# Attention and FFN on one core: the values product in parts between the two heads' transposes, scores of both heads first

## The chip, the core and the metric

One core of a Trainium2 chip runs the whole program. The time is device microseconds from launch to end; the median of three runs is compared. The span in a profile is the time between the first and the last instruction of one profiled execution.

## What is computed

Multi-head attention (batch 4, 8 heads, 576 positions, head width 64) with a position bias from a small network, then per batch a feed-forward layer with a convolution over three positions and a gate:

```python
scores = scale * q @ k.T + bias[h, i, j]        # bias = relu(x[i,j] * w1 + b1) @ w2
attn   = softmax(scores)                        # over j
x      = attn @ v                               # heads side by side: 4 x 576 x 512
h      = relu(x @ w_in)                         # 512 -> 1024
out    = (h * sigmoid(conv3(h))) @ w_out        # 1024 -> 512
```

All is float32 in and out.

## The kernel before

There are three stages: the bias table is computed and written to DRAM (to about 65 us in the profile), the attention runs (to about 328 us), then the feed-forward layer.

**Sequences and units.** The attention works on 16 sequences n, one for each pair of heads p and batch b. A sequence has five units, named by their row tile t, in the order t = 1, 2, 3, 4, 0 (`units`); below they are unit 0 to unit 4 by their place ui in that order. Units 0 to 3 hold 128 query rows for each of two heads h; unit 4 (t = 0) holds the remaining 64 rows of both heads in one tile. The loop `for u, (n, t) in enumerate(flat)` near the end of the printed code is software-pipelined over units: in pass u it issues

- `scores` of unit u+2 for head h: on TensorE (L341) into a PSUM tile `s` (pool psS, two tiles), then on VectorE (L348) the bias sum and the row minimum in one instruction, into `sp` and `nm`;
- `expo` of unit u+1 for head h: ScalarE's exponential (L362);
- `transposes` of unit u for head h: TensorE (L397) turns the 128 x 576 block into two PSUM tiles `tp` (pool psT, three tiles), one of which ScalarE copies to `pt` and the other VectorE (L88 and L91). ScalarE writes two columns of `sr` (L323) ahead of the first head's transposes.

**The values product.** When a group of row tiles is complete, `pv_parts` puts five parts on the list `fill`; a part is one block of 128 keys, both heads, and is two matmuls (L441) that accumulate in PSUM, 256 columns wide for a group of two tiles and 64 for unit 4's group. After the last part ScalarE copies the sum to `x` (L88). How many parts a pass takes off the list, at its end, is the table `pv_share`.

**Normalising.** `invert(n-1)` gives the reciprocals of the row sums on VectorE; two more transposes (L404) in unit 2 turn them, VectorE copies them to `rt`, and `normalise` sends them over the SyncE queue (SP) to DRAM (`r_d`, L472 to L474) and back, spread over partitions (`rb`, L477). At the end of unit 4 GpSimd (POOL) multiplies `x` by `rb` (L483).

**Weights beside it.** Each weight piece of the feed-forward layer is a job of `job_steps`, whose steps are called after each head's transposes over two units: L96 on ScalarE and L97 on VectorE, L99, L103, then GpSimd splits the piece (L130, L131). L97 of a job writes a buffer that GpSimd's L131 of the job before has to have read. A job's L97 falls into every second unit: for even n into unit 1 of the next sequence after GpSimd's L483, for odd n into unit 2.

**Loads.** All go over SP, in the order of the code: `load(n+2)` (queries and keys, four DMAs of 928 KB in all, L149 and L150) in unit 2, after the last scores of sequence n; `load_v` (values, four DMAs of 448 KB, L164 to L167) into one of two fixed tiles; the weight pieces (L118); and in every fourth sequence the five bias tiles of the next pair of heads (L175, L177). The DMAs take eight completion semaphores in turn, so one waits for the eighth before it to land.

Of the kernel before, what the change touches and what calls it, by code (L numbers as in the profile page):

```python
# [19 lines left out]
def attention_ffn_kernel(  # L20
# [63 lines left out]
    NSEQ = len(seq)  # L84
# [5 lines left out]
    def dve(o, i):  # L90
        nc.vector.tensor_copy(o, i)  # L91
# [25 lines left out]
    def load_w(raw, src):  # L117
        nc.sync.dma_start(raw.rearrange("p n t -> p (n t)"), src.bitcast(I32))  # L118
# [14 lines left out]
    with tc.manual_schedule():  # L133
# [27 lines left out]
        def load_v(n):  # L161
            p, b = seq[n]
            vts[n] = vt = v_t[n % 2]
            nc.sync.dma_start(vt[0:TL, 1:], v[b, p, 0:TL])  # L164
            nc.sync.dma_start(vt[TL:P, 6:], v[b, p, TL:P, 5:])
            nc.sync.dma_start(vt[TL:P, 1:5], v[b, p, TL:P, 0:4])
            nc.sync.dma_start(vt[TL:P, 0], v[b, p, TL:P, 4])  # L167
# [153 lines left out]
        def turned_sp(n, t):  # L321
            tile = sp_p.tile([P, 2 * S + 2], F32R, name="sr", tag=spt[n, t][1])
            nc.scalar.activation(tile[:, 2 * S:], pars[:, 0:2], AF.Copy)  # L323
            spt[n, t] = (tile, None)
# [34 lines left out]
        def expo(n, t, h):  # L359
            sp, nm = spt[n, t][0], nms[n, t]  # L360
            col = 4 * h + t - 1 if t else 8
            exps[n, t, h] = nc.scalar.activation(  # L362
                sp[:, h], sp[:, h], AF.Exp, bias=nm[:, h:h + 1], scale=-1.0,
                accum_out=sms[n][:, col:col + 1],
            )
# [3 lines left out]
        def group(n, t):  # L369
            return t if n == 0 and t > 2 else (t + 1) // 2  # L370

        def ends_group(n, t):
            return t in (0, 2, 4) or n == 0 and t == 3

        def transposes(n, t, h, sums=None):
            g = group(n, t)
            if (n, g) not in ptt:
                ptt[n, g] = pt_p.tile([P, 9, 2 * P], F32, name="pt") if g else pt0s[n % 2]
            pt = ptt[n, g]
            c0 = P if t == 2 or t == 4 and n else 0  # L380
            if h == 0:
                turned_sp(n, t)
            spf = spt[n, t][0]


            last = h or not t
            rows = P if t else TL
            blocks = [(4 * h + c, (5 * h + c) * P, P) for c in range(4)]
            if last:
                blocks.insert(4 - 4 * h, (8 if t else 4, NM, P if n or t else TL))  # L390


            ps = [psT.tile([P, 512], F32, name="tp").rearrange("p (c x) -> p c x", x=TL) for _ in range(2)]
            halves_ = [slice(TL * a, TL * a + TL) for a in range(2)]
            for k, (bk, j, cols) in enumerate(blocks):
                for a, ra in enumerate(halves_):
                    tr = nc.tensor.transpose(  # L397
                        ps[a][0:cols, bk - 4 * h].bitcast(F32R), spf[ra, j:j + cols], identr[ra, ra]
                    )
                    if k == 0 and a == 0:  # L400
                        tc.add_manual_dep(tr.ins, exps.pop((n, t, h)).ins.name, DATA)
            if sums is not None:
                for a, ra in enumerate(halves_):
                    nc.tensor.transpose(ps[a][:, 5], rr_t[sums % 2][ra], ident[ra, ra])  # L404
            for a, copy in ((0, act), (1, dve)):
                cs = slice(c0 + TL * a, c0 + TL * a + TL)
                if rows == P:
                    copy(pt[:, 4 * h:4 * h + len(blocks), cs], ps[a][:, 0:len(blocks)])
                else:
                    copy(pt[:, 0:4, cs], ps[a][:, 0:4])  # L410
                    copy(pt[0:rows, 4, cs], ps[a][0:rows, 4])
            if sums is not None:
                rts[sums] = r_p.tile([9, P], F32, name="rt")
                for a, ra in enumerate(halves_):
                    dve(rts[sums][:, ra], ps[a][0:9, 5])
# [81 lines left out]
        def ffn_in(b, f):  # L497
            ps = psS.tile([P, 2, 512], F32, name="s")
            cs = slice(f * P, f * P + P)
            i = 0  # L500
            for c in range(KC):
                for pw, px in ((0, 0), (0, 1), (1, 0)):
                    for a in range(2):
                        nc.tensor.matmul(  # L504
                            ps[:, a, 0:HS],
                            wi[c][:, pw, cs],
                            xss[b, c][:, px, a * HS:(a + 1) * HS],
                            start=(i == 0),
                            stop=(i == 3 * KC - 1),
                        )  # L510
                    i += 1
            if (b, f) in ((0, 0), (0, 1)):
                h = e_p.tile([P, S], F32, name="h")
            else:
                h = g_p[0].tile([P, S], F32, name="h", tag="g")
            nc.scalar.activation(halves(h), ps[:, :, 0:HS], AF.Relu)  # L516
            return h
# [35 lines left out]
        def heads(t):  # L553
            return (0, 1) if t else (0,)

        fill = deque()
# [42 lines left out]
        for u in range(2):  # L599
            for h in heads(flat[u][1]):  # L600
                scores(*flat[u], h)
            if u == 0:
                for h in heads(flat[0][1]):
                    expo(*flat[0], h)
        pv_share = (5, 0, 5, 0, 5)
        rb = None
        hs_ff = {}
        raw_w = {}
        job_steps = iter(())
# [3 lines left out]
        for u, (n, t) in enumerate(flat):  # L613
            p, b = seq[n]
            ui = units.index(t)
            for h in range(2):
                if u + 2 < NU:
                    if h in heads(flat[u + 2][1]):
                        scores(*flat[u + 2], h)
                if u + 1 < NU and h in heads(flat[u + 1][1]):  # L620
                    expo(*flat[u + 1], h)
                if h in heads(t):
                    transposes(n, t, h, n - 1 if h and ui == 2 and n else None)
                next(job_steps, None)
            del spt[n, t]
            if u + 2 >= NU:
                f = u + 2 - NU
                hs_ff[0, f] = ffn_in(0, f)
            if u == 1 or n and ui == 2 and n + 2 < NSEQ:
                load(2 if u == 1 else n + 2)  # L630
            if ui == (1 if n > 1 else 3) and 1 <= n and n + 1 < NSEQ:
                load_v(n + 1)
            if u in conv_weights:
                conv_weights[u]()

            for at, do in ((u - 8, "load"), (u - 11, "split")):
                job = at // 2
                if at % 2 == 0 or not 0 <= job < 4 * KC + 2 * FE:
                    continue
                if job < 4 * KC:  # L640
                    src, dst = w_in[job // 4 * P:job // 4 * P + P], wi[job // 4]
                else:
                    src, dst = w_out[(job - 4 * KC) // 2 * P:(job - 4 * KC) // 2 * P + P], wo[(job - 4 * KC) // 2]
                cs = slice(job % 4 * 256, job % 4 * 256 + 256) if job < 4 * KC else slice(job % 2 * 256, job % 2 * 256 + 256)
                if do == "load":
                    raw_w[job] = e_p.tile([P, 256, 2], I32, name="raw_w", tag="h")
                    load_w(raw_w[job], src[:, cs])
                else:
                    job_steps = split_w_steps(e_p, dst[:, :, cs], raw_w.pop(job), ("cv", "cv"))
            if u + 2 < NU:  # L650
                n2, t2 = flat[u + 2]
                p2, b2 = seq[n2]
                if b2 == B - 1 and p2 + 1 < NP:
                    load_bias(p2 + 1, t2)
            if ui == (0 if n > 1 else 1) and n > 0:
                invert(n - 1)

            parts = len(fill) if u < 4 else pv_share[ui]
            while fill and parts > 0:
                fill.popleft()()  # L660
                parts -= 1
            if ui == 2 and n > 0:
                rb = normalise(n - 1)
            if ends_group(n, t):
                fill.extend(pv_parts(n, group(n, t)))
            if ui == 4 and n > 0:
                apply_norm(n - 1, rb)
            if n == NSEQ - 2 and ui > 1:
                x_parts(0, ui - 2)
            if n == NSEQ - 1 and ui == 0:  # L670
                x_parts(0, 3)
            if n == NSEQ - 1 and ui in (1, 2):
                load_wo(FE - 1 + ui)
# [84 lines left out]
        for i, (b, f) in enumerate(steps):  # L758
# [12 lines left out]
            for c in range(KC):  # L771
# [5 lines left out]
                lambda f, gi, t=t: gs[b, f][:, gi, t * P:(t + 1) * P] for t in range(NT)  # L777
# [98 lines left out]
```

## Time and profile before

| | |
|---|---|
| runs (three) | 537.38 us median, 532.86 to 539.75 |
| profiled execution | 535.1 us, its span 533.3 us |
| mean granted TensorE clock | 0.991 |
| attention's full stretch on TensorE, 80 to 320 us | 225.59 us of 240 busy |
| ScalarE, VectorE, GpSimd over the span | 58%, 72%, 19% busy |

A row of the timeline reads: start, duration, engine, line, operation, output<-inputs, partitions x elements, count of records merged, and in brackets the engine's idle time just before with what ended it. A float32 matmul stands as two records. A matmul's end is modelled and overlaps the next one's start, so the cost of a step on TensorE is taken from start to start.

### The profile page before, as it was taken

What the parts mean: (1) busy time and instruction counts of PE and PEld (TensorE: products, weight loads), DVE (VectorE), ACT (ScalarE), POOL (GpSimd) and SP (SyncE); (2) the same over time, 40 slices, a digit from 0 to 9 for tenths busy, and PEclk for the clock granted to TensorE, in tenths of its full rate; (3) what the DMA queues carried; (4) which work ended last, traced back from release to release, by engine and by line L of the source; (5) the groups of instructions that cost most, each with busy time, mean ns of one, the idle gap of its engine ahead of it and who ended that gap; (6) DMA issues with size and microseconds to landing.
All of it is one profiled execution on the core that took longest, in us unless ns stands there. A gap on an engine that the chain in (4) does not pass through costs nothing.

```text
span 533.3 us, 11854 instructions
## 1 busy us (share of the span) xinstructions
PE 498.9 (94%) x4542; PEld 382.3 (72%) x4542; DVE 386.1 (72%) x919; ACT 311.6 (58%) x813; POOL 103.3 (19%) x123
## 2 busy tenths in 40 slices
PE   5989999999899999999889999899999999999995
PEld 2333466776667766677666678888998899899984
DVE  6999685677768777878678853995699169928910
ACT  6888785687757777677676654562362035215510
POOL 1000000012221222212222521562016001500000
PEclk9999999999989999999999999989999999999999
DMA  6689644597656976569754121000200200020011
GB/s 168 248 244 352 233 118 125 144 279 188 159 135 148 293 178 164 144 162 296 177 140 116 58 76 42 8 1 3 77 2 0 80 22 0 1 81 0 1 39 61
DMA packets 32707, 63.50 MB, mean 119 GB/s; under 512 B 5490, under 2 KB 11146, under 8 KB 32650
## 3 DMA queue, kind: packets, MB, share of 16 engines
q1 hardware_dynamic: 32506, 62.66, 41.1%
q8 instruction: 36, 0.59, 0.5%
q14 instruction: 21, 0.17, 0.1%
q10 hardware_dynamic: 144, 0.08, 0.1%
HBM read 46.74 MB, written 15.98 MB: 118 GB/s over the span
## 4 chain that ended last, share of the span: by engine, by line
PE 57%; DMA 11%; ACT 7%; DVE 6%; POOL 2%; issue 2%; SPq 1%; POOLq 0%; DVEq 0%; ACTq 0%
PE s L504 17%; PE tp L727 14%; PE o L441 10%; PE s L341 7%; PE tp L397 5%; PE o L727 4%; ACT sp L362 3%; DMA qk<-in_qk_dram 3%; DMA r_d<-rt 3%; DMA rb<-r_d 3%; DMA bt<-bias_d 2%; ACT pt L88 2%; POOL x L483 1%; DVE cv L702 1%; DVE sp L348 1%
## 5 line engine op out<-in xcount | busy, mean ns | idle before, releaser
L348 DVE CUSTOM_DVE_ANT_0 sp<-s,bt 128x576 f32<-128x576 f32 x144 | 107.8, 750 | 50.6 <-PE s L341 41.2
L397 PE MATMUL tp<-identr,sr 64*128 64x64 f32 x1312 | 110.7, 265 | 14.0 <-ACT pt L88 7.6
L341 PE MATMUL s<-qk 64*128 64x288 f32 x640 | 119.3, 449 | 1.2 <-DVE nm L348 1.1
L362 ACT ACTIVATE sp<-sp,nm 128x576 f32<-128x576 f32 x144 | 110.9, 770 | 3.5 <-DVE nm L348 3.4
L397 PEld LDWEIGHTS tp<-identr,sr 64*128 64x128 f32 x1312 | 78.3, 136 | 42.3 <-ACT pt L88 20.4
L504 PE MATMUL s<-xs,wi 128*128 128x288 f32 x768 | 105.2, 299 | 2.7 <-ACT h L516 2.7
L504 PEld LDWEIGHTS s<-xs,wi 128*128 128x128 f32 x768 | 104.1, 191 | 3.4 <-ACT h L516 2.9
L441 PE MATMUL o<-pt,vt 128*64 128x256 f32 (+2 forms) x940 | 88.6, 336 | 0.7 <-ACT x L88 0.7
L88 ACT ACTIVATE pt<-tp 128x256 f32<-128x256 f32 (+2 forms) x160 | 59.3, 381 | 39.0 <-PE tp L397 38.0
L441 PEld LDWEIGHTS o<-pt,vt 128*64 128x64 f32 x940 | 53.4, 138 | 26.9 <-issue 6.5
L91 DVE COPY pt<-tp 128x256 f32<-128x256 f32 (+2 forms) x160 | 66.5, 424 | 7.3 <-PE tp L397 6.8
L727 PE MATMUL tp<-wo,g 128*128 128x512 f32 x288 | 70.1, 389 | 0.0
L341 PEld LDWEIGHTS s<-qk 64*128 64x128 f32 x640 | 54.1, 185 | 19.6 <-issue 6.1
L702 DVE SCALAR_TENSOR_TENSOR cv<-h,cw,cv 128x575 f32<-128x575 f32 x64 | 60.8, 950 | 2.4 <-ACT cv L697 0.4
L727 PEld LDWEIGHTS tp<-wo,g 128*128 128x128 f32 x288 | 53.8, 188 | 11.0
L483 POOL TENSOR_TENSOR x<-x,rb 128x576 f32<-128x576 f32 x16 | 22.8, 1423 | 184.7 <-DMA rb<-r_d 169.3
L260 PE MATMUL s<-y,pars 128*32 128x512 f32 (+8 forms) x352 | 46.0, 494 | 4.6 <-ACT st L286 2.0
L243 DVE TENSOR_SCALAR y<-tl,inv,nb 128x512 f32<-128x512 f32 (+8 forms) x116 | 49.9, 502 | 0.0
L516 ACT ACTIVATE h<-s 128x576 f32<-128x576 f32 x32 | 20.8, 650 | 47.2 <-PE s L504 47.1
L708 ACT ACTIVATE cv<-cv 128x576 f32<-128x576 f32 x32 | 21.8, 682 | 29.5 <-DVE cv L702 29.5
L260 PEld LDWEIGHTS s<-y,pars 128*32 128x32 f32 x352 | 15.2, 111 | 28.9 <-DVE y L243 13.6
L130 POOL TENSOR_SCALAR xs<-x 128x576 fp32r<-128x576 f32 x16 | 15.3, 954 | 82.0 <-PE s L504 82.0
(66 smaller groups left out, 456.5 us busy)
## 6 DMA issues: line engine op xcount, KB each, us to landing
qk<-in_qk_dram SPq DMA_DIRECT2D x32, 320.0 KB
bt<-bias_d SPq DMA_DIRECT2D x32, 288.0 KB
bias_d<-st SPq DMA_DIRECT2D x14, 607.0 KB
qk<-in_qk_dram SPq DMA_DIRECT2D x32, 144.0 KB
rb<-r_d SPq DMA_DIRECT2D x32, 144.0 KB
out_dram<-o SPq DMA_DIRECT2D x17, 256.0 KB
raw_w<-in_moe_w_in_dram SPq DMA_DIRECT2D x16, 256.0 KB
vt<-in_v_dram SPq DMA_DIRECT2D x16, 224.0 KB
```

What stands on the lines that cost most here:

```text
L88: nc.scalar.activation(o, i, AF.Copy)
L91: nc.vector.tensor_copy(o, i)
L243: nc.vector.tensor_scalar(y, dist[:, 0:n], inv[:, ig:ig + 1], nb1, op0=ALU.mult, op1=ALU.max)
L260: nc.tensor.matmul(ps[32 * j:32 * j + 32, a // 512 if n > 512 else blk % 2, 0:min(n - a, 512)], w2b, ys[j][:, a:min(n, a + 512)], start=Tr ...
L341: nc.tensor.matmul(ps[:, a, 0:HS], qt[rows, qo:qo + P], qt[rows, KO + hh * HS:KO + hh * HS + HS], start=(i == 0), stop=(i == len(ops) - 1),)
L348: nc.vector.tensor_tensor_reduce(out=halves(spt[n, t][0][:, h]), in0=ps[:, :, 0:HS], in1=halves(bt[:, h]), op0=ALU.add, op1=ALU.min, scale ...
L362: exps[n, t, h] = nc.scalar.activation(sp[:, h], sp[:, h], AF.Exp, bias=nm[:, h:h + 1], scale=-1.0, accum_out=sms[n][:, col:col + 1],)
L397: tr = nc.tensor.transpose(ps[a][0:cols, bk - 4 * h].bitcast(F32R), spf[ra, j:j + cols], identr[ra, ra])
L441: nc.tensor.matmul(po[hs, oc], vt[:, slot, :], rhs, start=(c == 0), stop=(c == 4))
L504: nc.tensor.matmul(ps[:, a, 0:HS], wi[c][:, pw, cs], xss[b, c][:, px, a * HS:(a + 1) * HS], start=(i == 0), stop=(i == 3 * KC - 1),)
L702: nc.vector.scalar_tensor_tensor(out=cv[:, o:o + S - 1], in0=h[:, i:i + S - 1], scalar=cw[:, f, kk:kk + 1], in1=cv[:, o:o + S - 1], op0=AL ...
L727: nc.tensor.matmul(ps, lhs(f, gi), wo[f][:, wj, cs], start=(f == 0 and i == 0), stop=(f == FC - 1 and i == 2),)
```

## The change

For each pass the scores of both heads of unit u+2, and the exponentials of both heads of unit u+1, are issued first. Then come the first head's transposes, then the pass's parts of the values product, then the second head's transposes. The product's parts go 2, 5, 3, 2, 3 to units 0 to 4 instead of 5, 0, 5, 0, 5. For n > 1 the values are loaded in unit 2 instead of unit 1, behind `load(n+2)` and the bias, ahead of `normalise`. Nothing is computed differently.

```diff
-        pv_share = (5, 0, 5, 0, 5)
+        pv_share = (2, 5, 3, 2, 3)
...
             for h in range(2):
                 if u + 2 < NU:
                     if h in heads(flat[u + 2][1]):
                         scores(*flat[u + 2], h)
                 if u + 1 < NU and h in heads(flat[u + 1][1]):
                     expo(*flat[u + 1], h)
-                if h in heads(t):
-                    transposes(n, t, h, n - 1 if h and ui == 2 and n else None)
-                next(job_steps, None)
+            transposes(n, t, 0)
+            next(job_steps, None)
+
+            parts = len(fill) if u < 5 else pv_share[ui]
+            while fill and parts > 0:
+                fill.popleft()()
+                parts -= 1
+            if t:
+                transposes(n, t, 1, n - 1 if ui == 2 and n else None)
+            next(job_steps, None)
...
-            if ui == (1 if n > 1 else 3) and 1 <= n and n + 1 < NSEQ:
-                load_v(n + 1)
...
             if ui == (0 if n > 1 else 1) and n > 0:
                 invert(n - 1)
-
-            parts = len(fill) if u < 4 else pv_share[ui]
-            while fill and parts > 0:
-                fill.popleft()()
-                parts -= 1
+            if ui == (2 if n > 1 else 3) and 1 <= n and n + 1 < NSEQ:
+                load_v(n + 1)
             if ui == 2 and n > 0:
                 rb = normalise(n - 1)
```

TensorE, units 0 and 1 of one sequence, before (`s` scores, `tp` transposes, `o` the values product; x2 is one head's scores, x10 five parts):

```order
L341 MATMUL s<-qk 128x288 x2
L397 MATMUL tp<-identr,sr 128x64 x8
L341 MATMUL s<-qk 128x288 x2
L397 MATMUL tp<-identr,sr 128x64 x10
L441 MATMUL o<-pt_161,vt_107 64x64 x10
L341 MATMUL s<-qk 128x288 x2
L397 MATMUL tp<-identr,sr 128x64 x8
L341 MATMUL s<-qk 128x288 x2
L397 MATMUL tp<-identr,sr 128x64 x10
```

The same two units on TensorE now:

```order
L341 MATMUL s<-qk 128x288 x4
L397 MATMUL tp<-identr,sr 128x64 x8
L441 MATMUL o<-pt,vt_107 64x256 x4
L397 MATMUL tp<-identr,sr 128x64 x10
L341 MATMUL s<-qk 128x288 x4
L397 MATMUL tp<-identr,sr 128x64 x8
L441 MATMUL o<-pt_161,vt_107 64x64 x10
L397 MATMUL tp<-identr,sr 128x64 x10
```

Both units now have a piece of the product between their two sets of transposes, where before only the scores of the second head stood.

ScalarE in unit 1, before (`sp` exponentials, `pt` copies of the transposes, `u` a step of a weight job):

```order
L362 ACTIVATE sp,sm<-sp,nm 128x576
L323 ACTIVATE sr<-pars 128x2
L88 ACTIVATE pt<-tp 128x4x64
L96 ACTIVATE u<-raw_w 128x256
L362 ACTIVATE sp,sm<-sp,nm 128x576
L88 ACTIVATE pt<-tp 128x5x64
```

The same unit on ScalarE now (`x` is the copy of the short product, which stood at the end of unit 0):

```order
L362 ACTIVATE sp,sm<-sp,nm 128x576 x2
L323 ACTIVATE sr<-pars 128x2
L88 ACTIVATE pt<-tp 128x4x64
L88 ACTIVATE x_1585<-o 128x64
L88 ACTIVATE pt<-tp 128x5x64
```

The copy of the first head's transposes stands behind two exponentials instead of one, and no exponential is left between the two copies.

SP from unit 1 to unit 2 of a sequence, before (`vt` values, `qk` queries and keys, `r_d` the reciprocals on their way to DRAM):

```order
L164 DMA vt_107<-in_v_dram 64x896
L165 DMA vt_107<-in_v_dram 64x576
L166 DMA vt_107<-in_v_dram 64x256
L167 DMA vt_107<-in_v_dram 64x64
L149 DMA qk<-in_qk_dram 64x1280
L150 DMA qk<-in_qk_dram 64x2x288
L149 DMA qk<-in_qk_dram 64x1280
L150 DMA qk<-in_qk_dram 64x2x288
L118 DMA raw_w<-in_moe_w_in_dram 128x512
L472 DMA r_d<-rt 4x128
L473 DMA r_d<-rt 4x128
L474 DMA r_d<-rt 2x1x64
```

The same twelve on SP now:

```order
L149 DMA qk<-in_qk_dram 64x1280
L150 DMA qk<-in_qk_dram 64x2x288
L149 DMA qk<-in_qk_dram 64x1280
L150 DMA qk<-in_qk_dram 64x2x288
L118 DMA raw_w<-in_moe_w_in_dram 128x512
L164 DMA vt_107<-in_v_dram 64x896
L165 DMA vt_107<-in_v_dram 64x576
L166 DMA vt_107<-in_v_dram 64x256
L167 DMA vt_107<-in_v_dram 64x64
L472 DMA r_d<-rt 4x128
L473 DMA r_d<-rt 4x128
L474 DMA r_d<-rt 2x1x64
```

The four loads of the values have moved from ahead of the queries and keys to just ahead of the reciprocals.

## Rows read from the trace of the kernel before

**Rows 1.** The page's first part: each engine's busy time, share of the span and number of instructions.

```profile
PE 498.9 (94%) x4542; PEld 382.3 (72%) x4542; DVE 386.1 (72%) x919; ACT 311.6 (58%) x813; POOL 103.3 (19%) x123
```

**Rows 2.** Timeline of TensorE: the values product in unit 2, of sequence 2 and of sequence 15 (the first and the last of 14).

```profile
98.14 2.38 PE L441 MATMUL o<-pt,vt 128*64 128x256 f32 x20
...
313.18 2.38 PE L441 MATMUL o<-pt,vt 128*64 128x256 f32 x20
```

**Rows 3.** Timeline of TensorE in one sequence, from the product in unit 2 of sequence 9 to the same place of sequence 10.

```profile
214.56 2.38 PE L441 MATMUL o<-pt,vt 128*64 128x256 f32 x20
216.86 0.76 PE L341 MATMUL s<-qk 64*128 64x288 f32 x4
217.24 0.64 PE L397 MATMUL tp<-identr,sr 64*128 64x64 f32 x8
217.72 0.75 PE L341 MATMUL s<-qk 64*128 64x288 f32 x4
218.09 0.84 PE L397 MATMUL tp<-identr,sr 64*128 64x64 f32 x10
218.69 0.75 PE L341 MATMUL s<-qk 64*128 64x288 f32 x3
...
219.73 0.82 PE L341 MATMUL s<-qk 64*128 64x288 f32 x4
220.48 2.38 PE L441 MATMUL o<-pt,vt 128*64 128x256 f32 x20
...
224.67 0.58 PE L397 MATMUL tp<-identr,sr 64*128 64x64 f32 x9 [0.26 <-ACT pt L88]
225.19 0.80 PE L441 MATMUL o<-pt,vt 128*64 128x64 f32 x20
...
230.09 0.35 PE L404 MATMUL tp<-ident,rr 64*128 64x64 f32 x2
230.37 1.95 PE L441 MATMUL o<-pt,vt 128*64 128x256 f32 x16
```

**Rows 4.** Timeline of ScalarE and VectorE in the same sequence.

```profile
217.69 0.76 DVE L348 CUSTOM_DVE_ANT_0 sp<-s,bt 128x576 f32<-128x576 f32 x1 [1.49 <-PE s L341]
...
218.38 0.42 DVE L91 COPY pt<-tp 128x256 f32<-128x256 f32 x1
218.71 0.29 DVE L97 TENSOR_SCALAR w<-raw_w 128x256 int32<-128x256 int32 x1
...
224.25 0.37 ACT L88 ACTIVATE pt<-tp 128x256 f32<-128x256 f32 x1
...
226.16 0.77 ACT L362 ACTIVATE sp<-sp,nm 128x576 f32<-128x576 f32 x1
...
227.01 0.37 ACT L88 ACTIVATE pt<-tp 128x256 f32<-128x256 f32 x1
...
228.03 0.43 ACT L88 ACTIVATE pt<-tp 128x320 f32<-128x320 f32 x1
```

**Rows 5.** Timeline of several engines in sequence 10, which loads no bias: the last scores of the sequence, the queries' load behind them, the way of the reciprocals over SP, GpSimd's multiplication and the split that follows it, and the next job's first step on VectorE.

```profile
227.78 1.23 PE L341 MATMUL s<-qk 64*128 64x288 f32 x7
...
229.12 0.47 SPq L149 DMA_DIRECT2D qk<-in_qk_dram  x1
...
232.30 0.28 SPq L472 DMA_DIRECT2D r_d<-rt  x1
...
237.04 1.13 SPq L477 DMA_DIRECT2D rb<-r_d  x2
...
240.91 1.41 POOL L483 TENSOR_TENSOR x<-x,rb 128x576 f32<-128x576 f32 x1 [4.67 <-DMA rb<-r_d]
...
242.78 0.73 POOL L131 TENSOR_TENSOR wo<-w,wo 128x256 fp32r<-128x256 f32 x1
...
243.73 0.28 DVE L97 TENSOR_SCALAR w<-raw_w 128x256 int32<-128x256 int32 x1
```

**Rows 6.** Timeline of VectorE: all rows of L97 that waited for GpSimd.

```profile
132.07 0.30 DVE L97 TENSOR_SCALAR w<-raw_w 128x256 int32<-128x256 int32 x1 [2.12 <-POOL wi L131]
...
145.93 0.29 DVE L97 TENSOR_SCALAR w<-raw_w 128x256 int32<-128x256 int32 x1 [2.15 <-POOL wi L131]
...
199.80 0.29 DVE L97 TENSOR_SCALAR w<-raw_w 128x256 int32<-128x256 int32 x1 [2.50 <-POOL wi L131]
...
212.50 0.29 DVE L97 TENSOR_SCALAR w<-raw_w 128x256 int32<-128x256 int32 x1 [1.21 <-POOL wi L131]
...
265.50 0.29 DVE L97 TENSOR_SCALAR w<-raw_w 128x256 int32<-128x256 int32 x1 [3.26 <-POOL wo L131]
...
278.39 0.29 DVE L97 TENSOR_SCALAR w<-raw_w 128x256 int32<-128x256 int32 x1 [1.39 <-POOL wo L131]
```

**Rows 7.** Timeline of TensorE at its three longest waits for VectorE in the attention, and one row of the windows view (from:to, length, then busy time and records of TensorE, its weight loads, VectorE, ScalarE, GpSimd, the granted clock, DMA share, GB/s).

```profile
147.36 0.59 PE L397 MATMUL tp<-identr,sr 64*128 64x64 f32 x10 [2.15 <-DVE pt L91]
147.98 3.88 PE L441 MATMUL o<-pt,vt 128*64 128x256 f32 x20
...
213.93 0.58 PE L397 MATMUL tp<-identr,sr 64*128 64x64 f32 x10 [1.22 <-DVE pt L91]
...
279.82 0.59 PE L397 MATMUL tp<-identr,sr 64*128 64x64 f32 x10 [1.40 <-DVE pt L91]
...
150.00:151.00 1.00, 1.00 (x8) 0.63 (x6) 0.00 (x0) 0.00 (x0) 0.28 (x1) 0.50 0.98 197
```

## The prediction, made before the change was run

> **What bounds the kernel now.** I read the page's busy shares first: TensorE is busy 94% of the span [rows 1]. That says little by itself, so I went to TensorE's timeline in the attention, the only stage that the change touches. From sequence 2 to sequence 15 the values product of unit 2 begins 13 periods apart, at 98.14 and 313.18 [rows 2]: 215.04 / 13 = 16.54 us a sequence. One undisturbed sequence, 214.56 to 230.37, takes 15.81 [rows 3].
>
> What must TensorE do in one? From start to start [rows 3]: scores of a head 0.37 (217.72 to 218.09), transposes of a first head 0.48 (217.24 to 217.72), of a second 0.60 (218.09 to 218.69), the row sums 0.28 (230.09 to 230.37), five wide parts of the product 2.30 (214.56 to 216.86), or 0.46 each, and five narrow ones 0.80. Ten scores (unit 4 counts double for its two operands) are 3.70, four first heads and five with five blocks 4.92, sums 0.28, products 5.40: 14.30. So 1.5 of 15.81 us is waiting. It lies in two kinds of place: TensorE waits for a copy that frees a `tp` tile (0.26 shown at 224.67, and more in the modelled ends), and the product after scores starts 0.75 after them instead of 0.37 (219.73 to 220.48).
>
> The rest of the 16.54 is something else. Three times TensorE stands for 2.15, 1.22 and 1.40 us, and after the first the next product takes 3.88 instead of 2.38, with a granted clock of 0.50, the 1.2 GHz level [rows 7]. That is 6.3 us in all. The waits view by line and VectorE's timeline show whence: VectorE's L97 stands for GpSimd's split of the job before [rows 6], and GpSimd stands, with the multiplication L483 ahead of that split in its queue, for the reciprocals to come back by DMA [rows 5]. So in these places the bound is a chain through SP, DMA, GpSimd and VectorE.
>
> **The change part by part.**
>
> *TensorE's order.* The work stays 14.30. Each unit now has a piece of product between its transposes, so the copies of the first head are made under it. The product no longer follows scores, and that 0.38 goes.
>
> *ScalarE's order.* Here a new wait comes. The second head's transposes need a `tp` tile that ScalarE's copy of the first head frees, and this copy now stands behind both exponentials. ScalarE's loop through one unit is: copy of the second head 0.43, exponential 0.77, exponential with the `sr` write 0.85 (226.16 to 227.01), copy of the first head 0.37, then the hand-over to TensorE 0.05 (224.25 + 0.37 to 224.67), then the second transposes 0.58, before the next copy can start [rows 3, 4]: 3.05. Before, the second exponential ran under these transposes; now ScalarE has nothing there. TensorE's own time from one second transposes to the next, with the new shares, is 0.60 + 0.74 + 0.48 + 0.80 = 2.62 in unit 1, 0.60 + 0.74 + 0.48 + 1.38 = 3.20 in unit 2, 0.88 + 0.74 + 0.48 + 0.92 = 3.02 in unit 3 (where ScalarE has one exponential only), and 5.46 over units 4 and 0 (ScalarE about 5.1). So only unit 1 is held, by 3.05 - 2.62 = 0.43. The period becomes 14.73, or 1.08 less than 15.81.
>
> *VectorE.* Its score step can start 0.83 after the scores do (216.86 to 217.69), takes 0.69, a copy 0.33 [rows 3, 4]. Two steps, two copies and half a job are about 2.6 a unit, under TensorE's 2.7 to 3.2, and the scores tiles are freed nearly a unit ahead. I charge nothing; the cover is a tenth of a microsecond in units 0 and 1, and a further 0.1 a unit there would cost 13 x 0.2 = 2.6.
>
> Without any wait of the chain, 13 periods would fall from 215.04 to 13 x 14.73 = 191.5, by 23.5, and sequence 1, with nearly the same five units, by another 1.1.
>
> *The loads on SP.* This part works against the rest. The values' four DMAs now stand between the queries and the reciprocals. In sequence 10 the queries start at 229.12, the reciprocals are issued at 232.30, and `rb` at 237.04, since it waits for them to land [rows 5]. So the four or five DMAs ahead hold them up for about 8 us from the queries' start. Four issues more cost SP some 2.5 (five took 232.30 - 229.12 = 3.2). By bytes: 928 + 256 KB in the 7.9 us to 237.04 is 150 KB a us, so 448 KB more are up to 3.0. At the other end, if SP was waiting and the transfers run side by side, nothing. I take 2.0, nearer to the end that the shown sequence supports.
>
> What does 2.0 cost? In sequence 10 the chain runs from the last scores, 227.78, to the split's end, 242.78 + 0.73: 15.73, and L97 begins at 243.73 without a wait, 0.2 to spare [rows 5]. In the new order L97 is wanted earlier: the rest of unit 2 (3.48), units 3, 4 and 0 (2.74 + 2.72 + 2.74) and in unit 1 the score steps and a copy (0.83 + 0.69 + 0.69 + 0.33) make 14.2, with some lag of VectorE 14.4. The chain is then 17.7, so VectorE stands 3.3. Behind L97 waits the copy of the second head, and the product part in unit 2 needs it; TensorE has about 0.5 before it gets there, so it loses 2.8. Sequences 6 and 10 are of this kind (even, with a job, no bias load before): 5.6.
>
> Sequences 3, 4, 7, 8, 11 and 12 follow the bias loads and waited already, in pairs (2.12 and 2.15, 2.50 and 1.21, 3.26 and 1.39) [rows 6]. There the queue was full, so I take the DMAs' order as worth nothing, but the units come 1.1 sooner per period. The first wait of a pair lies in unit 2. It was hidden under a whole product of 2.30; now only 1.38 of product and what follows, some 1.2 beyond VectorE's own work, hides it. A pair with waits f and s costs TensorE f + 1.1 - 1.2 at first; the second, 2.2 late less what was lost already and 0.5, brings it to the larger of f - 0.1 and s + 1.7: 3.85, 2.91 and 3.16, in all 9.9. In a bias sequence a values load ahead of the reciprocals may add up to 3.0 to each pair.
>
> *The clock.* A stand of 2.15 was followed by 1.5 us lost at the lower clock; those of 1.22 and 1.40 were not [rows 7]. Some five stands will be above 2. I charge two of them, 3.0, with bounds of 0 and 8 x 1.5 = 12.
>
> *Sum.* 535.1 - 23.5 - 1.1 + 5.6 + 9.9 + 3.0 = 529.0 for a profiled execution. The 6.3 us of old waits are inside the 23.5. The median of the runs before is 2.3 above the profiled execution, so about half of that on top gives 530.
>
> **A rule that speaks against it.** The trace shows the product starting 0.75 after the start of scores, where transposes follow scores after 0.37 [rows 3]; after nine transposes it starts after 0.52 (224.67 to 225.19), no later than transposes would. The Trainium skill ("TensorEngine Tiling (Array Packing)", Key Properties) says that changing the tiling mode drains TensorE. Scores and transposes use 64 rows, the product 64 columns, and the number of such changes rises from six to ten a sequence. The one row after transposes shows no price; what a change from the product into transposes costs, no row shows. That is the third case below.
>
> **The rivals.**
>
> *The chain does not stretch.* If the values run beside the queries, and the old waits stay at 6.3, the sum is 535.1 - 23.5 - 1.1 + 6.3 = 516.8. For it: these DMAs spread over all engines of the queue. Against: `rb` waited 4.7 us after the reciprocals were issued, behind loads of the very kind that is now added.
>
> *Turning round costs.* Four products now lead into transposes. At 0.38 each, as after scores, the period is 14.73 + 1.52 = 16.25, 0.44 above 15.81. The chain has more time then: sequences 6 and 10 lose 1.3 each, the old 6.3 stay, and the sum is 535.1 + 13 x 0.44 + 2.6 = 543.4; at half the price some 535. For it: the scores' rows. Against: scores stream 288 columns through each half, transposes 64.
>
> *Slower: the reciprocals' way becomes the bound.* Place: L97 on VectorE behind GpSimd. Price: with 3.0 of delay in every sequence the two stands are 3.8 each, the three pairs 9.9 + 9.0, and the lower clock follows all eight, 12.0: 535.1 - 24.6 + 7.6 + 18.9 + 12.0 = 549.0. With every stand followed by the lower clock it decides from about 0.2 of delay on in all eight: 24.6 - 12.0 - 9.9 leaves 2.7, the two stands take 1.7 of it at no delay, and each further microsecond costs 5; with the two clock losses of the forecast it takes 2.0. For it: [rows 5, 6]. Against: in full queues the order moves little.
>
> **How the numbers follow.** The forecast gets 0.45, the unstretched chain 0.28, the turning round 0.15, the slower case 0.12. Measurement of this kernel tells about 2% (10.7 us) from no change. The unstretched chain is faster by more than that, and a twentieth of the forecast's spread: 0.33. The slower case is beyond 2% but for its lower part: 0.11. The rest is 0.56. The range goes from the unstretched chain to the full price of turning round, 516 to 543; the forecast's own range is 523 to 537.
>
> **What would show it.** Right: start-to-start of the product in unit 2 below 15 us where VectorE's L97 doesn't wait; in unit 1 the second transposes waiting some 0.4 for ScalarE's copy; the reciprocals' row on SP 5 to 6 us after the queries' instead of 3.2; L97 waiting for GpSimd in sequences 6 and 10 too; stands of 2 us and more on TensorE, some with a granted clock of 0.50 behind them. Wrong: L97 without new waits (then the faster case), transposes that start late behind a product with no copy outstanding (turning round), or unit times above 3.1 us with VectorE never idle, which would mean that its thin cover was gone.

## The result and the profile after

The changed kernel takes 541.08 us median (537.73 to 545.77), the kernel before 537.32: a ratio of 1.0069, between 1.0043 and 1.0096. The change is a small loss, clear of the noise, where a gain to 530 was forecast. The profiled execution takes 545.77 us, 10.7 more than that of before. It is the slowest of the changed kernel's 20 runs, 4.7 above their median, and its mean granted clock of 0.971 is the lowest of them (0.971 to 0.983).

TensorE's timeline in the changed kernel, at the row sums' transposes (L404, once per sequence): sequences 2, 3 and 15.

```profile
99.15 0.27 PE L404 MATMUL tp<-ident,rr 64*128 64x64 f32 x2
...
114.17 0.28 PE L404 MATMUL tp<-ident,rr 64*128 64x64 f32 x2
...
323.03 0.28 PE L404 MATMUL tp<-ident,rr 64*128 64x64 f32 x2
```

From 2 to 3 is 15.02 us, an undisturbed period, against 15.81 before [rows 3] (15.82 and 16.09 in turn over the other quiet sequences). So the new order does give something. But the 13 periods come to 223.88, against 215.04 [rows 2]: 13 x 15.02 is 195.3, and 28.6 us are lost in single places. The same timeline shows them, and VectorE's shows L97 in the same places (answering to [rows 6, 7]):

```profile
129.05 1.61 PE L441 MATMUL o<-pt,vt 128*64 128x256 f32 x12 [1.65 <-DMA vt<-in_v_dram]
...
137.69 0.69 PE L397 MATMUL tp<-identr,sr 64*128 64x64 f32 x7 [5.35 <-DVE rt L91]
...
186.12 2.82 PE L441 MATMUL o<-pt,vt 128*64 128x256 f32 x10 [2.89 <-DVE pt L91]
...
221.93 2.26 PE L441 MATMUL o<-pt,vt 128*64 128x256 f32 x10 [2.37 <-DVE pt L91]
...
256.75 2.82 PE L441 MATMUL o<-pt,vt 128*64 128x256 f32 x10 [2.44 <-DVE pt L91]
...
277.93 0.50 PE L397 MATMUL tp<-identr,sr 64*128 64x64 f32 x7 [1.47 <-DVE rt L91]
```

```profile
136.82 0.29 DVE L97 TENSOR_SCALAR w<-raw_w 128x256 int32<-128x256 int32 x1 [7.70 <-POOL wi L131]
...
185.37 0.29 DVE L97 TENSOR_SCALAR w<-raw_w 128x256 int32<-128x256 int32 x1 [4.46 <-POOL wi L131]
...
221.19 0.29 DVE L97 TENSOR_SCALAR w<-raw_w 128x256 int32<-128x256 int32 x1 [3.94 <-POOL wi L131]
...
256.00 0.29 DVE L97 TENSOR_SCALAR w<-raw_w 128x256 int32<-128x256 int32 x1 [4.01 <-POOL wo L131]
...
277.07 0.29 DVE L97 TENSOR_SCALAR w<-raw_w 128x256 int32<-128x256 int32 x1 [2.75 <-POOL wo L131]
```

Each stand of TensorE but the first comes just behind a late L97. Timeline of SP and GpSimd ahead of the one at 256 us (the chain of [rows 5], again in sequence 10):

```profile
238.33 0.48 SPq L149 DMA_DIRECT2D qk<-in_qk_dram  x1
...
243.97 0.43 SPq L472 DMA_DIRECT2D r_d<-rt  x1
...
249.01 1.12 SPq L477 DMA_DIRECT2D rb<-r_d  x2
...
253.38 1.41 POOL L483 TENSOR_TENSOR x<-x,rb 128x576 f32<-128x576 f32 x1 [8.10 <-DMA rb<-r_d]
...
255.24 0.73 POOL L131 TENSOR_TENSOR wo<-w,wo 128x256 fp32r<-128x256 f32 x1
```

From the queries' issue the reciprocals are issued after 5.64 us (before 3.18), their return after 10.68 (7.92), and the split ends after 17.64 (14.39). So the return is issued 2.76 later, the split ends 3.25 later, and it is wanted sooner.

The windows view shows what follows two of these stands (columns as in [rows 7]; the granted clock is the third number from the end):

```profile
138.00:140.00 2.00, 2.00 (x14) 1.01 (x11) 2.00 (x7) 0.38 (x1) 0.00 (x0) 0.50 0.85 194
140.00:142.00 2.00, 2.00 (x18) 1.49 (x18) 0.61 (x2) 0.93 (x2) 1.14 (x2) 0.50 0.93 223
...
258.00:260.00 2.00, 2.00 (x14) 0.97 (x10) 0.37 (x2) 0.00 (x0) 1.13 (x2) 0.50 0.99 324
260.00:262.00 2.00, 2.00 (x28) 1.73 (x28) 1.54 (x6) 1.58 (x6) 0.00 (x0) 0.98 1.02 305
```

TensorE is busy in all four rows, but in the first three at 1.2 GHz.

### The profile page after: what moved, and what is told of

It reads as the page before. It is cut to its first block, busy times and chain, and to the rows that moved or that the text cites. A ratio compares the mean times of both kernels' runs of the same rounds, so it can differ in the third digit from the quotient of the medians.

```text
span 543.9 us, 11908 instructions
## 1 busy us (share of the span) xinstructions
PE 503.7 (93%) x4542; PEld 389.3 (72%) x4542; DVE 389.1 (72%) x919; ACT 313.5 (58%) x813; POOL 103.4 (19%) x123
## 4 chain that ended last, share of the span: by engine, by line
PE 58%; DMA 12%; DVE 5%; ACT 5%; POOL 3%; SPq 2%; issue 1%; POOLq 0%; DVEq 0%
PE s L504 16%; PE tp L729 14%; PE o L441 10%; PE s L341 7%; PE tp L397 6%; PE o L729 4%; DMA rb<-r_d 4%; DMA qk<-in_qk_dram 4%; DMA r_d<-rt 3%; ACT sp L362 2%; POOL x L483 2%; DVE cv L704 1%; ACT pt L88 1%; DMA bt<-bias_d 1%; ACT x L88 1%
## 5 line engine op out<-in xcount | busy, mean ns | idle before, releaser
L348 DVE CUSTOM_DVE_ANT_0 sp<-s,bt 128x576 f32<-128x576 f32 x144 | 103.6, 750 | 22.2 <-PE s L341 11.4
L441 PE MATMUL o<-pt,vt 128*64 128x256 f32 (+2 forms) x940 | 100.7, 344 | 10.1 <-DVE pt L91 7.7
L504 PE MATMUL s<-xs,wi 128*128 128x288 f32 x768 | 106.6, 301 | 2.7 <-ACT h L516 2.7
L504 PEld LDWEIGHTS s<-xs,wi 128*128 128x128 f32 x768 | 105.4, 193 | 3.7 <-ACT h L516 2.9
L397 PE MATMUL tp<-identr,sr 64*128 64x64 f32 x1312 | 97.0, 264 | 11.5 <-DVE rt L91 7.6
L397 PEld LDWEIGHTS tp<-identr,sr 64*128 64x128 f32 x1312 | 75.0, 138 | 44.5 <-issue 20.5
L341 PE MATMUL s<-qk 64*128 64x288 f32 x640 | 103.2, 437 | 0.7 <-DVE nm L348 0.6
L341 PEld LDWEIGHTS s<-qk 64*128 64x128 f32 x640 | 59.7, 193 | 18.2 <-DVE pt L91 4.6
L483 POOL TENSOR_TENSOR x<-x,rb 128x576 f32<-128x576 f32 x16 | 22.8, 1425 | 206.5 <-ACT pt L88 101.6
```

Of the source, the lines that this page charges most:

```text
L341: nc.tensor.matmul(ps[:, a, 0:HS], qt[rows, qo:qo + P], qt[rows, KO + hh * HS:KO + hh * HS + HS], start=(i == 0), stop=(i == len(ops) - 1),)
L348: nc.vector.tensor_tensor_reduce(out=halves(spt[n, t][0][:, h]), in0=ps[:, :, 0:HS], in1=halves(bt[:, h]), op0=ALU.add, op1=ALU.min, scale ...
L397: tr = nc.tensor.transpose(ps[a][0:cols, bk - 4 * h].bitcast(F32R), spf[ra, j:j + cols], identr[ra, ra])
L441: nc.tensor.matmul(po[hs, oc], vt[:, slot, :], rhs, start=(c == 0), stop=(c == 4))
L504: nc.tensor.matmul(ps[:, a, 0:HS], wi[c][:, pw, cs], xss[b, c][:, px, a * HS:(a + 1) * HS], start=(i == 0), stop=(i == 3 * KC - 1),)
```

## The experiments

Theory A: the reciprocals' way (SP, DMA, GpSimd's L483 ahead of the split, L97) eats what the order gains. Theory B: the order itself costs what it gains. The periods of all kernels, from TensorE's timeline (L404 to L404, in the profiled execution; the time is the median of the runs, and the profiled execution can lie some us from it, 534.18 against 539.6 for e3). The last three columns are the longer period of each pair behind a bias load: 3 to 4 or 4 to 5, 7 to 8 or 8 to 9, 11 to 12 or 12 to 13.

| kernel | time, us | undisturbed | 13 periods | bias 1 | bias 2 | bias 3 |
|---|---|---|---|---|---|---|
| before | 537.3 | 15.82, 16.09 | 215.05 | 18.05 | 17.28 | 18.23 |
| changed | 541.1 | 15.02 | 223.88 | 23.38 | 19.11 | 17.46 |
| e1_values_first | 536.9 | 15.02 | 217.65 | 23.11 | 22.17 | 20.85 |
| e2_loads_alone | 547.3 | 15.82 | 227.03 | 21.52 | 18.40 | 19.35 |
| e3_late_normalising | 539.6 | 15.03 | 213.39 | 19.60 | 18.06 | 20.91 |
| e4_before_late_norm | 529.3 | 15.81, 16.10 | 209.20 | 17.07 | 16.10 | 16.10 |
| e5_both | 533.8 | 15.03 | 213.26 | 22.28 | 19.33 | 20.30 |
| e6_exp_later | 531.9 | 14.63 | 212.26 | 23.21 | 17.43 | 22.03 |
| e7_product_last | 563.8 | 18.18 | 236.39 | 18.18 | 18.19 | 18.20 |
| e8_reciprocals_first | 555.2 | none | 231.60 | 20.83 | 20.96 | 21.73 |
| e9_late_return | 512.5 | 14.63 | 193.14 | 14.95 | 14.67 | 14.97 |
| e10_return_e5 | 518.0 | 15.03 | 196.58 | 15.04 | 15.18 | 15.02 |
| e11_return_e3 | 522.6 | 15.02 | 203.25 | 19.28 | 17.20 | 15.04 |
| e12_return_e4 | 528.5 | 15.82, 16.10 | 208.26 | 16.11 | 16.10 | 16.11 |

**e1_values_first**: the loads' part undone.

```diff
+            if ui == (1 if n > 1 else 3) and 1 <= n and n + 1 < NSEQ:
+                load_v(n + 1)
             if u in conv_weights:
...
-            if ui == (2 if n > 1 else 3) and 1 <= n and n + 1 < NSEQ:
-                load_v(n + 1)
             if ui == 2 and n > 0:
                 rb = normalise(n - 1)
```

> The changed kernel with one thing put back: the values' four loads stand in unit 1 again, ahead of the queries and the bias, instead of between the bias and the reciprocals. The order of the work stays the new one. Theory A (the reciprocals' way eats the gain): L97's waits for GpSimd of 4.46, 3.94 and 4.01 us near 185, 221 and 256 us fall to below 2, TensorE's wait of 1.65 for the values' tile goes, and with them most of the lower clock: 529 us, between 521 and 533. Theory B (the order itself costs, by turning round or by ScalarE's longer loop): the loads' place is worth nothing, 538 to 542. An undisturbed period is 15.0 in both.

536.92 us, ratio 1.0018 (0.9983 to 1.0053). In sequences 6 and 10 L97 waits 1.18 and 1.67 now and the periods are 15.32 and 15.76, as A says; TensorE's wait for the values is gone. But the three bias periods hold 21.1 us above 15.02 (L97 waits 5.29 there for its weight piece's load, then 5.43 and 3.73 for GpSimd): the order alone, with loads as before, neither wins nor loses. The time lies outside both forecasts (521 to 533, and 538 to 542): A is half right, and it missed what is left there.

**e2_loads_alone**: the same lines the other way, in the kernel before.

> The kernel before with the loads' part of the change alone: the values are loaded in unit 2 ahead of the reciprocals; the order of TensorE and ScalarE is the old one. Theory A: L97 waits 1 to 2 us in sequences 6 and 10, where it did not wait, and 1 to 3 more in each pair after a bias load, with some more of the lower clock: 541 to 548 us, middle 544. Theory B: 537, within 2.

547.34 us, ratio 1.0222 (1.0153 to 1.0291). A, at the upper end: moving four loads ahead of the reciprocals costs some 2% in the old order. L97 waits 2.17 and 1.83 for GpSimd in sequences 6 and 10, and TensorE stands for VectorE just behind:

```profile
184.60 0.82 PE L397 MATMUL tp<-identr,sr 64*128 64x64 f32 x10 [2.18 <-DVE pt L91]
...
255.95 0.82 PE L397 MATMUL tp<-identr,sr 64*128 64x64 f32 x10 [1.84 <-DVE pt L91]
```

**e3_late_normalising** (changed kernel) and **e4_before_late_norm** (kernel before): L483 goes behind the split in GpSimd's queue.

```diff
-            if ui == 4 and n > 0:
+            if ui == 4 and n == NSEQ - 1:
                 apply_norm(n - 1, rb)
+            if ui == 1 and n > 1:
+                apply_norm(n - 2, rb)
```

> The changed kernel with GpSimd's multiplication L483 issued two units later (in unit 1 of the next sequence, behind the split of the job instead of ahead of it), so that the reciprocals' way no longer stands ahead of the split. Loads and order stay as changed. Theory A: L97's waits for GpSimd go below 1 us, the granted clock stays at 2.4 GHz outside the values' wait, and 13 periods come to 13 x 15.0 + 2 to 5: 514 to 521 us. Theory B: 538 to 542, since the chain was not what cost.

> The kernel before with the same shift of L483 into unit 1 of the next sequence. Theory A: its stands of 2.15, 1.22 and 1.40 and the 1.5 of lower clock go: 529 to 533 us. Theory B: these stands have another cause behind GpSimd, 536 to 538.

e4: 529.33 us, ratio 0.9883 (0.9829 to 0.9937), as A says. e3: 539.60 us, ratio 1.0003 (0.9953 to 1.0053), runs from 532.72 to 542.50, and that is a miss for A: no L97 waits for GpSimd now, but VectorE's timeline shows another releaser, the weight piece's own load, and TensorE's shows the values' tile.

```profile
132.65 0.29 DVE L97 TENSOR_SCALAR w<-raw_w 128x256 int32<-128x256 int32 x1 [3.96 <-DMA raw_w<-in_moe_w_in_dram]
...
199.46 0.71 DVE L97 TENSOR_SCALAR w<-raw_w 128x256 int32<-128x256 int32 x1 [4.78 <-DMA raw_w<-in_moe_w_in_dram]
```

```profile
194.46 2.21 PE L441 MATMUL o<-pt,vt 128*64 128x256 f32 x12 [2.06 <-DMA vt<-in_v_dram]
```

**e5_both**: the edits of e1 and e3 together.

> The changed order with the values' loads back in unit 1 and L483 behind the split: the order alone, with the reciprocals' way taken out of the split's. It stands against the kernel before with the late L483 (529.3 us), from which it differs by the order only. Its quiet period was 15.95 there (15.81 and 16.10 in turn), and is 15.02 in the changed order: 13 x 0.93 = 12.1 less. Theory A: 517 us, up to 523 if a weight piece that comes late behind the bias tiles still stops L97. Theory B (the order itself costs what it gains): 528 or more.

533.78 us, ratio 0.9872 (0.9806 to 0.9939): above A's range, inside B's (528 or more), and no better than e4 (0.9883), from which it differs by the order with the shorter period. Nearly all of the loss (16.8 us over three periods) is in the bias columns. The chain that ended last shows what held the first (cut):

```profile
129.94 4.52 DMA raw_w<-in_moe_w_in_dram
...
134.58 0.84 DVE w L97
135.41 0.40 DVE pt L91
135.81 0.13 DVE rt L91
...
135.99 0.70 PE tp L397 x6
```

and SP's timeline why the weight piece was issued at 129.94 only:

```profile
125.01 0.61 SPq L474 DMA_DIRECT2D r_d<-rt  x1
128.71 1.12 SPq L477 DMA_DIRECT2D rb<-r_d  x2
129.94 0.99 SPq L118 DMA_DIRECT2D raw_w<-in_moe_w_in_dram  x2
```

SP stands at L477 for 3.1 us (125.62 to 128.71) until the reciprocals have landed, with the weight pieces behind it (SyncE's waits view puts 43.0 us over 17 times to L477 waiting for `r_d`). In the other two bias periods it stands there for 1.4 and 2.7 us, again ahead of the weight pieces. So the same wait seems to reach L97 by a second way, which does not pass GpSimd; e9 and e10 test it.

**e6_exp_later** (on e5_both): `expo` of the second head moves behind the first head's transposes.

> As e5_both, with the second head's exponential issued behind the first head's transposes and copy, as in the kernel before, so that ScalarE's copy is no longer behind both exponentials. Theory A with ScalarE's loop as the limit of unit 1: the 0.4 us that the second transposes wait there go, period 14.6, 5 us less than e5_both. Rival: VectorE or the exponential for the next unit is late instead, and the time stays within 2 us of e5_both or rises.

531.89 us, ratio 0.9832 (0.9759 to 0.9905). The undisturbed period falls by 0.40, to 14.63: ScalarE's loop was that much of unit 1, as A says. But the 13 periods fall by 1.0 only, where 13 x 0.40 is 5.2, and the time by 1.9, within the 2 us of the rival. The bias periods take 2.0 of it back, and the periods 6 to 7, 10 to 11 and 14 to 15 most of the rest (15.18, 15.37 and 16.50).

**e7_product_last** (on e5_both): the product's parts move behind the second head's transposes.

> As e5_both, but each pass's parts of the product stand behind the second head's transposes, as before, with the new shares 2, 5, 3, 2, 3. If the copies hidden under the product bring the gain, the period goes back to about 15.9 and the time to 528; if scores of both heads first bring it, it stays at 15.0 and 517.

563.77 us, ratio 1.0442 (1.0382 to 1.0502): a period of 18.18, beyond both guesses. With scores of both heads first and nothing between the two sets of transposes, each second set waits for ScalarE's copy (39.3 us over 62 waits in the waits view). So scores of both heads first pay only with a piece of the product between the two sets.

**e8_reciprocals_first** (changed kernel): `normalise(n - 1)` moves ahead of `load(n + 2)`.

> The changed kernel with the reciprocals' way (L472 to L477) issued ahead of the queries, the bias and the values in unit 2, instead of behind them; L483 stays ahead of the split. Theory A: the reciprocals come back some 5 us sooner, L97 does not wait for GpSimd any more, the time is 520 to 530 us, unless the queries, which now stand behind the wait for the reciprocals on SP, come late. Rival (the queue is full whatever the order): waits and time as in the changed kernel, 537 to 542.

555.24 us, ratio 1.0292 (1.0221 to 1.0363): a miss for both. The return follows the last reciprocals sooner, but SP now stands for the sums to be turned and for the landing with every load behind it, and the values come late (20.5 us in 12 waits of TensorE). SP's timeline from the last load of one sequence to the first of the next: from 95.58 it issues nothing for 8.3 us.

```profile
95.04 0.54 SPq L167 DMA_DIRECT2D vt<-in_v_dram  x1
103.89 0.26 SPq L472 DMA_DIRECT2D r_d<-rt  x1
...
104.54 0.63 SPq L474 DMA_DIRECT2D r_d<-rt  x1
106.23 1.12 SPq L477 DMA_DIRECT2D rb<-r_d  x2
107.44 0.54 SPq L149 DMA_DIRECT2D qk<-in_qk_dram  x1
```

That gave A its second form: whatever stands on SP behind the wait for the reciprocals comes late.

**e9_late_return**, **e10_return_e5**, **e11_return_e3**, **e12_return_e4**: the return load alone goes to unit 4, behind that pass's weight piece, in e6, e5, e3 and e4.

```diff
+        def fetch(n):
             rb = rb_p.tile([P, S], F32, name="rb")
...
             if ui == 2 and n > 0:
-                rb = normalise(n - 1)
+                normalise(n - 1)
+            if ui == (4 if n < NSEQ - 1 else 2) and n > 0:
+                rb = fetch(n - 1)
```

> As e6_exp_later, with the reciprocals' return load (L477) issued two units later, in unit 4 behind that pass's weight piece, so that SP does not stand for the reciprocals to land with the weight piece queued behind it. In e6_exp_later three periods of 23.21, 17.43 and 22.03 hold the whole excess over 14.63 (L97 waiting for the weight piece's DMA). Theory A in its second form (any load queued on SP behind the wait for the reciprocals comes late): these fall to 15 to 17, 13 periods to about 195, time 512 to 519. Rival (the DMA engines are full after a bias load, the order on SP is worth nothing): 528 to 532.

> As e5_both, with the same later return load. Its three periods of 22.28, 19.33 and 20.30 fall to 15 to 17: 13 periods of 15.02 are 195.3, time 515 to 521. Rival as for e9_late_return: 530 to 534.

> As e3_late_normalising (the values' loads in unit 2, as changed), with the later return load: with nothing behind it on SP that waits for the reciprocals, the loads' place should be worth little, but for the 2.9 us in which TensorE waits for the values' tile: 516 to 525. Rival: 530 or more, the loads' place costs by itself.

> As e4_before_late_norm (the order of before), with the later return load: only its 1.3 us in period 4 can go, 527 to 529. It is the old order with no wait for the reciprocals in any queue, against e10_return_e5, which differs by the order alone: 13 x 0.93 = 12 us between them by the quiet periods.

512.48 us, ratio 0.9540 (0.9474 to 0.9606); 518.04, 0.9644 (0.9585 to 0.9703); 522.62, 0.9727 (0.9661 to 0.9794); 528.45, 0.9841 (0.9784 to 0.9898). All four lie where A's second form has them; the rival's ranges, given for the first three, are missed. e12 is hardly below e4 (0.9883), as forecast: the old order had little left to free. In e9 SP's timeline shows the weight piece ahead of the return, and VectorE's shows L97 without a wait in the place where e6 waited 5.61:

```profile
121.96 0.36 SPq L118 DMA_DIRECT2D raw_w<-in_moe_w_in_dram  x1
124.20 1.12 SPq L479 DMA_DIRECT2D rb<-r_d  x2
```

```profile
126.56 0.28 DVE L97 TENSOR_SCALAR w<-raw_w 128x256 int32<-128x256 int32 x1
```

e10 and e12 differ by the order alone: 10.4 us, where the undisturbed periods gave 12. That is against B: free of the waits, the order gains 2%. e11 against e10 is the loads' place once the return is issued later: 4.6 us. The expected wait for the values' tile is not there; what is left is the reciprocals' way again. L97 waits 3.79 and 3.06 for GpSimd in two bias periods, and in the first of them GpSimd's multiplication starts 9.6 us after the return's issue among the bias tiles (108.73 to 118.37), having waited for it. e9 beats both kernels, the one before by 4.6%, the changed one by some 5%; it holds the order (but for one exponential), not the loads' part, and two edits that the change did not have.

## Why the prediction was wrong

The profiled execution was put at 529.0 and took 545.8, 16.8 more (the median is 541.1 against 530). The step that failed most is the clock's: it was charged 3.0 for two stands and took 9.1 behind four, and these 6.1 are the whole forecast gain of the profiled execution (535.1 - 529.0). TensorE's period, 0.29 too short in the forecast, and smaller terms make the loss. Step by step:

- *TensorE's order.* Direction right; the period is 15.02, not 14.73: 13 x 0.29 = 3.8. The wait of unit 1 is there (303.91 below, 0.40 behind 303.51) and e6 measures it as 0.40, forecast 0.43. What was missed lies in the other steps. The changed kernel's TensorE, units 3 to 1 of sequence 13 to 14:

```profile
294.09 1.08 PE L441 MATMUL o<-pt,vt 128*64 128x256 f32 x8
295.11 0.58 PE L397 MATMUL tp<-identr,sr 64*128 64x64 f32 x10
295.52 1.24 PE L341 MATMUL s<-qk 64*128 64x288 f32 x8
296.38 0.72 PE L397 MATMUL tp<-identr,sr 64*128 64x64 f32 x10
297.03 1.52 PE L441 MATMUL o<-pt,vt 128*64 128x256 f32 x12
298.48 1.24 PE L341 MATMUL s<-qk 64*128 64x288 f32 x8
299.34 0.64 PE L397 MATMUL tp<-identr,sr 64*128 64x64 f32 x8
299.91 1.08 PE L441 MATMUL o<-pt,vt 128*64 128x256 f32 x8
...
302.77 0.80 PE L441 MATMUL o<-pt,vt 128*64 128x64 f32 x20
303.51 0.25 PE L397 MATMUL tp<-identr,sr 64*128 64x64 f32 x1
303.91 0.58 PE L397 MATMUL tp<-identr,sr 64*128 64x64 f32 x9 [0.15 <-ACT pt L88]
```

  From start to start, two wide parts take 1.02 instead of 0.92 and three 1.45 instead of 1.38, the scores of both heads 0.86 instead of 0.74, a first head's transposes ahead of a product 0.57 instead of 0.48. On the other side a second head's transposes ahead of scores take 0.41 instead of 0.60, the row sums 0.11 instead of 0.28, the narrow product 0.74 instead of 0.80. Over a sequence these add up to some 1.4 us one way and 1.0 the other, and the net is the 0.3. As a matmul's end is modelled, a price can show in a step or in its neighbour, so which of these changes pays it is not shown.

  This also bears on *turning round costs*. The 0.3 is under 0.1 for each of the four more changes of tiling, and a product in pieces is followed 0.07 to 0.10 later, not 0.38. That case fell; that its time (543.4) lies nearest to the measured one is luck, and its sum was high: over the mean of the two quiet periods before (15.82 and 16.09) its 16.25 is 0.30 more, not 0.44, which makes it some 2 us less. The Trainium skill ("TensorEngine Tiling (Array Packing)", Key Properties) is borne out at most to that size.
- *Sequence 1 and what follows the periods.* L404 of sequence 2 starts 1.3 later than before (99.15 against 97.86), but it is no mark from one kernel to the other: three parts of the product that stood behind it [rows 3] now stand ahead of it. A mark that stands at the same place in both is L466, the last sequence's row sums, before and changed:

```profile
328.06 0.33 PE L466 MATMUL tp<-ident,rr 128*128 128x128 f32 x1
...
337.26 0.33 PE L466 MATMUL tp<-ident,rr 128*128 128x128 f32 x1
```

  It is 9.2 later; 8.8 of that are the 13 periods (223.88 against 215.05), so the rest of the attention lost 0.4 where a gain of 1.1 was forecast: 1.5. The feed-forward stage behind it, which the change does not touch and the forecast left alone, takes 1.4 more. Both kernels stand there for 2.7 us; before, the clock is up again soon after it, in the changed execution later (windows view, before and changed):

```profile
351.00:353.00 2.00, 2.00 (x14) 1.78 (x13) 2.00 (x3) 1.37 (x4) 1.92 (x2) 1.00 0.00 0
...
360.00:362.00 2.00, 2.00 (x10) 2.00 (x10) 2.00 (x3) 1.35 (x3) 1.92 (x2) 0.50 0.00 0
```

  These rows begin 3.8 and 3.6 us behind the first matmul after that stand (347.24 and 356.43).
- *The loads on SP.* The delay was 2.76 to the return's issue, for which 2.0 and a bound of 3.0 were worked out, and 3.25 to the split's end. The two stands in sequences without a bias load were put at 2.8 each: 2.89 and 2.44. The pairs, put at 9.9 in all, cost 5.35 + 2.37 + 1.47 = 9.2 by rows. The mechanism was right and the total well sized, though the split into pairs was not (3.85, 2.91 and 3.16 were put down). Missed beside it: TensorE's 1.65 for the values' own tile.
- *The clock.* This step failed. Charged 3.0, for two stands. Four stands of 2.4 us and more were followed by rows with a clock of 0.50, and their periods lose, beyond the stand, 3.0 (23.38 - 15.02 - 5.35), 2.2, 1.7 and 2.2: 9.1. The bound of 12 held it, the value taken did not; and I had said myself that some five stands would be above 2. Another 3.4 is spread over periods without a stand of that size; 1.1 of it lies in the period from 7 to 8, at whose start the clock is still 0.50 behind the stand at 186.12 (windows view, 190 to 191). All this is of one execution with the lowest clock of its kernel; what the clock takes in the median run is not shown.

The sum: 3.8 + 1.5 + 1.4 for the feed-forward stage + 6.1 for the clock + 1.65 + 3.4 - 1.0 for stands below forecast = 16.9, against 16.8.

*VectorE charged nothing* held: in e9, at a period of 14.63, no wait of TensorE for it in the attention is above 0.74. *The chain does not stretch* fell with e2. The *slower* case had the right place and the right sign; its clock (12.0) is nearer to the 9.1 than the forecast's 3.0, but its stands (7.6 and 18.9) were far too dear, 14.5 by rows, and its time, 549.0, lies beyond what was measured. Of the signs that I named the reciprocals' row 5.6 us behind the queries', L97 waiting in sequences 6 and 10, the 0.4 in unit 1 and the stands with a clock of 0.50 behind them were there; a period below 15 us was not (15.02).

The change itself was cut down by one cause in two ways. The order makes every sequence shorter, so what comes round over SP is wanted sooner, and the loads' part makes it come later. That the wait at L477 also held the weight pieces, I did not see before e3 and e5: [rows 6] name GpSimd alone, as there its split came last. In the changed kernel too every late L97 shown waits for GpSimd; the second way comes up in e1, once, and stands alone in e3 and e5.

Left open: why TensorE's own work is 0.3 longer in a sequence than was added up (pipeline or change of tiling), which no run tells apart, and the rest of the 3.4.

## What to carry to other kernels

When an order is tightened, list the loops that leave the engines (here sums to DRAM and back), and set their length against the new period before counting the gain. Behind a queue's instruction that waits for data, look at everything queued after it: undoing the wait at one reader (e3, e5) showed the next, and only taking the waiting instruction out of the way (e9) freed the gain. Charge a stand on TensorE with the clock that follows it: here 1.7 to 3.0 us for each stand of 2.4 to 5.4.

## What the runs showed of the hardware

A small transfer's round trip goes with what is queued: from the last reciprocals' issue to the return's issue on SP 1.7 us where no load stood ahead (e8, 104.54 to 106.23), and 3.5 to 3.7 behind loads (245.48 to 249.01 in the changed kernel, 125.01 to 128.71 in e5). In the changed kernel, after stands of 1.5 us (277.93) and 1.65 us (129.05), with a granted clock of 1.00 behind both, the periods lose 1.0 and 0.2 beyond the stand; after those of 2.4 and more, with 0.50 behind them, 1.7 to 3.0.
